# An 18-slot attention chain for the first two batches, one 512-column filler product, and weight conversions paced three then two per slot

## The chip, the cores and the metric

The kernel runs on one core of one Trainium2 chip. The metric is the device time of one execution in microseconds (us); smaller is better. The kernel before took 1901.67 us, the median of 3 runs that lie between 1897.96 and 1902.06. Engines: PE is TensorE (matmul), DVE is VectorE, ACT is ScalarE, POOL is GpSimd, SP is SyncE, which issues DMAs.

## The reference

For 8 batches of 8 heads, 576 tokens and head width 64, a Nystrom attention runs first: 32 landmarks per head are means of 18 tokens, three softmaxes (query by landmark, landmark by landmark, landmark by key), and a pseudo-inverse of the middle one by six Newton steps. Two feed-forward blocks follow on rows of 512.

```
A, Bm, C = sm(q, k_lm), sm(q_lm, k_lm), sm(q_lm, k)
for _ in range(6): Z = 2 * Z - Z @ Bm @ Z
x = (A @ Z @ C @ v)                      # heads side by side, 512 wide
u = x + (x.T @ U @ V).T ;  x = u + relu(u @ w_ch1) @ w_ch2
u = x + real(fft2(x))   ;  out = u + relu(norm(u) @ w2_ch1) @ w2_ch2
```

Each `w_ch1` is 512x2048 and each `w_ch2` is 2048x512. The weights come as 64-bit floats.

## The kernel before, in words

The two feed-forward blocks are four passes over all 8*576 columns: each pass takes half of the 2048 hidden rows. A pass goes through nine units of 512 columns. A unit has 8 "up" steps (`up`, L234) and 8 half "down" steps (L282 to L309), 16 steps in all, and every product is made of three MATMULs on a high and a low part (L241 to L243, L290 to L292). An up step ends in an ACT copy (L245) and a DVE subtraction (L246), which make the high and the low part of `g`.

The weights of the first pass are turned from 64-bit to two 32-bit parts on the chip, 16 pieces of 128x512, by `convert` (L90) under `direct` (L932). One piece has four sub-steps: (a) two DVE instructions, L96 and L97; (b) two on DVE, L100 and L103, one on ACT, L101, and one on POOL, L104; (c) one on DVE, L106, which needs L104; (d) a cast on ACT, L51, and a subtraction on POOL, L52. `direct` interleaves two pieces: a of piece n, c and d of piece n-1, b of piece n. The two small matrices U and V go through `from_f64` (L54) ahead of them, eight sub-steps.

The attention of a batch is a list of steps with slot numbers (`steps`, L664). A slot is the unit in which the kernel's code is written out: in each slot (loop at L996 before the feed-forward stream begins, loop at L1002 after it) first comes one step of the feed-forward stream or else a filler product (`filler`, L980), then the attention steps of that slot, then some conversion sub-steps. In the first loop the filler stands behind the attention steps. All engines run their instructions in the order in which they are written, so a slot is no time but a place in five queues.

Batch 0 begins at slot -21 and batch 1 at slot -10, each with 21 slots. The stream begins at slot 0. Its first unit is written in two halves and takes slots 0, 1, 2, 4, 6, 8, 9, 10; slots 3, 5 and 7 hold fillers. The second unit begins at slot 11, and from there every slot holds a stream step. Batch 2 begins at slot 4, and every later one 16 slots on.

The names that the prediction uses: `landmark` (L382, DVE L386), `kernel` and its normalisation (L410 to L428), `norms` (L434), `scores` (L458, MATMUL L468, maximum L476, exponentials L482 and L484), `query` (L527, DVE L552 and L553), `newton` (L603, L612 and L617), `rank` (L632, L641) and `mix` (L644), which gives the batch's rows, copies them (ACT L657) and splits them for the stream (ACT L51, DVE L52).

Of the kernel before, what the change touches and what calls it, by code (L numbers as in the profile page):

```python
# [20 lines left out]
B, H, S, D = 8, 8, 576, 64  # L21
DM, FF, R = 512, 2048, 32
LM, W = 32, 18
P = 128
# [15 lines left out]
def body(ctx: ExitStack, tc: tile.TileContext, qT, kT, vn, mU, mV, w11, w12, w21, w22,  # L40
         ident, bones, istack, tabs, out):
    nc = tc.nc
# [4 lines left out]
    ident_sb = const.tile([P, P], F32, name="ident_sb")  # L47
# [265 lines left out]
    STEPS = HM + 8  # L313
# [10 lines left out]
    def attention_constants(cp, t):  # L324
        nc.sync.dma_start(ident_sb, ident)
        t["U"] = cp.tile([P, 5, R], F32, name="U_sb")
        for nm in ("kb", "qb"):
            t[nm] = cp.tile([P, 4, 64], F32, name=nm)
            nc.gpsimd.memset(t[nm], 0.0)
        for nm, src, n in (("bones", bones, P), ("istack", istack, R)):  # L330
            t[nm] = cp.tile([P, n], F32, name=nm + "_sb")
            nc.sync.dma_start(t[nm], src)
        t["at"] = cp.tile([P, 4, S], F32, name="at")
        t["W"] = cp.tile([P, 4, 64], F32, name="W")
# [15 lines left out]
    def place_v(t):  # L350
        for n in range(3):
            src = t["vst"][R * n:R * n + R].unsqueeze(1).to_broadcast([R, 2, S // 3])
            for h in range(4):
                nc.sync.dma_start(t["at"][32 * h:32 * h + 32, 1 - h % 2:4:2, n * S // 3:(n + 1) * S // 3], src)

    class Batch:
# [307 lines left out]
        def steps(self, after):  # L664

            H0, H1 = slice(0, 512), slice(512, 1152)
            yield from ((2 * (nm == "q") + g, lambda nm=nm, g=g: self.landmark(nm, g)) for nm in "kq" for g in (0, 1))
            yield from ((5, self.kernel), (6, self.kernel_norm), (7, self.kernel_t), (8, self.norms), (9, self.residue))
            yield from ((10 + i, lambda i=i: self.newton(i)) for i in range(6))
            yield from ((6, self.scores), (8, lambda: self.query(0)), (9, lambda: self.query(1)),  # L670
                        (9, lambda: self.query_exp(H0)), (9, self.scores_sum), (10, lambda: self.scores_t(0)), (10, lambda: self.query(2)),
                        (11, lambda: self.scores_t(1)), (11, self.scores_tail), (11, lambda: self.query_exp(H1)),
                        (11, lambda: self.query_norm(H0)), (12, self.values), (12, lambda: self.query_norm(H1)),
                        (13, lambda: self.query_t(0)), (14, lambda: self.query_t(1)), (14, self.query_tail),
                        (15, self.mixed), (16, self.heads), (17, self.rank))
            if self.b:
                yield 13, lambda: self.mlp.get_tail(self.b)
                yield from ((15 + k // 2, lambda k=k: self.mlp.hand_tail(self.b, k)) for k in range(4))
            yield from ((19 + g, lambda g=g, n=n: self.mix(g, n)) for g in range(2) for n in range(2))
            if after:  # L680
                yield from ((r, lambda nm=nm: after.load(nm)) for r, nm in ((7, "k"), (10, "q"), (13, "v")))

        LAST = 20


    u2 = [dram.tile([DM, S], F32, name=f"u2_{b}") for b in range(B)]
# [30 lines left out]
    class Mixer:  # L717
# [170 lines left out]

        LAST = 28

    def pool(name, **k):
        return tc.tile_pool(name=name, bufs=1, reuse_waits="tile", **k)

    def chained(gens):
        for g in gens:
            yield from g

    def some(gen, n):
        for _ in range(n):
            next(gen, 0)  # L900

    class Slots:
# [5 lines left out]
        def add(self, first, steps):  # L908
            for r, step in steps:
                self.at.setdefault(first + r, []).append(step)  # L910
# [14 lines left out]
    def staging(cv, p, bufs=1):  # L925
        return chained([stage(cv, srcs[p][i], staged[p][i], bufs) for i in range(2 * HM)])

    N = NCH * STEPS
    with pool("mm") as mp, pool("pm", space=PSUM) as pm:
# [37 lines left out]
        with pool("aa") as ap_, pool("ac") as ac, pool("cv0") as cv0, pool("pt", space=PSUM) as psb:  # L967
            t = {}
            batches = [Batch(ap_, psb, t, b, mlp) for b in range(B)]
            slots = Slots()  # L970
            FIRST, GAP = -1 - Batch.LAST, 11
            half = (0, 1, 2, 4, 6, 8, 9, 10)
            for b in range(B):
                slots.add(GAP + STEPS * (b - 1) - 23 + 2 * (b == 1) if b else FIRST, batches[b].steps(batches[b + 1] if b + 1 < B else None))
            slots.add(GAP + STEPS * (B - 1) - 10, [(0, lambda: mlp.get_tail(B))])
            slots.add(GAP + STEPS * (B - 1) - 8, ((k, lambda k=k: mlp.hand_tail(B, k)) for k in range(4)))

            slots.add(FIRST, [(11, lambda: place_v(t))])

            def filler():  # L980

                ps = mlp.bank()
                for _ in range(6):
                    nc.tensor.matmul(ps[:, 0:P], ident_sb, ident_sb, start=True, stop=True)  # L984

            with tc.manual_schedule():
                for what in "kq":
                    batches[0].load(what)
                attention_constants(ac, t)
                small, large = attention_setup(t, ap_, cv0), direct()  # L990
                some(small, 1)
                some(large, 1)
                batches[0].load("v")
                some(large, 1)
                convs = chained([small, large])
                for s in range(FIRST, 0):  # L996
                    slots.run(s)
                    if s > FIRST + 5:
                        filler()
                    some(convs, 0 if s < FIRST + 4 else 1 + s % 2)  # L1000
                later, gen = staging(cv0, 1, 2), mlp.stream(0)
                for s in range(N + GAP - 8):  # L1002
                    if s >= GAP or s in half:
                        next(gen)
                    else:
                        filler()
                    slots.run(s)
                    if s < GAP + 13:
                        some(convs, 2)
                        if s == GAP + 12:  # L1010
                            some(convs, 99)
                    else:
                        some(later, 1 if s % 3 == 2 else 2)
                some(later, 999)
                some(gen, 9)
        with tc.manual_schedule(), pool("cv") as cv:
            with pool("fp") as fp, pool("fc") as fc, pool("pf", space=PSUM) as psb:
                f = {}
                slots = Slots()
# [97 lines left out]
```

## Time and profile before

| | |
|---|---|
| median of 3 runs | 1901.67 us |
| the profiled execution | 1898.48 us, of which 1896.7 us is the span from first to last instruction |
| PE busy | 1855.9 us (98%) |
| DVE, ACT, POOL busy | 914.0, 567.6, 377.4 us |
| mean granted clock of PE | 0.996 |

PE is busy nearly everywhere; its slices fall below 9 tenths at the start alone (the first slice, 47 us long, has 6). DVE is the other way round: its slices are 7, 8, 8, 6 in the first 190 us and then 6 or less. A place with a name helps to read the start: the first MATMUL of the second unit (L241, slot 11), which begins 112.73 us into the span.

### The profile page before, as it was taken

To read this page: it belongs to the slowest core of one execution; us is meant where nothing else is said; L and a number is where in the kernel's file an instruction comes from. 1 tells how busy PE (TensorE), PEld (TensorE's weight loads), DVE (VectorE), ACT (ScalarE), POOL (GpSimd) and SP (SyncE) were. 2 spreads that over 40 slices of the span, in tenths; PEclk is the share of its full clock that TensorE was granted. 3 is DMA by queue.
4 is the path that set the end of the run, shared out by engine and by line. 5 is a ranking of instruction groups with operands and counts; after the bars stand their busy time and mean duration, and the time that the engine had idled before them with its cause. 6 is when DMAs were issued, how large, how long until landed. Compare 5 with 4: busy or idle time off the path is not lost.

```text
span 1896.7 us, 30003 instructions
## 1 busy us (share of the span) xinstructions
PE 1855.9 (98%) x12184; PEld 1501.5 (79%) x12184; DVE 914.0 (48%) x1592; ACT 567.6 (30%) x1211; POOL 377.4 (20%) x354
## 2 busy tenths in 40 slices
PE   6999999999999999999999999999999999999998
PEld 5767777777788888887887888888888888888887
DVE  7886556556323434755645455464332133333333
ACT  3544443444212212323333243342322212111111
POOL 2333211221200222313222031332111000000000
PEclk9999999999999999999999999999999999999999
DMA  7454445442537343524536544252433733333332
GB/s 261 138 176 159 141 170 190 148 154 99 178 128 272 119 136 112 173 95 157 191 106 243 182 133 163 90 170 83 132 109 121 229 94 95 95 100 100 95 100 78
DMA packets 152922, 270.91 MB, mean 143 GB/s; under 512 B 23920, under 2 KB 82896, under 8 KB 152784
## 3 DMA queue, kind: packets, MB, share of 16 engines
q1 hardware_dynamic: 148176, 259.56, 40.8%
q10 hardware_dynamic: 4608, 9.44, 1.3%
q8 instruction: 95, 1.56, 0.3%
q14 instruction: 43, 0.35, 0.1%
HBM read 173.72 MB, written 94.63 MB: 141 GB/s over the span
## 4 chain that ended last, share of the span: by engine, by line
PE 88%; DVE 5%; DMA 2%; ACT 2%; issue 1%; SPq 0%; POOL 0%; ACTq 0%; DVEq 0%
PE ps L290 14%; PE ps L292 13%; PE ps L291 13%; PE ps L241 12%; PE ps L243 12%; PE ps L242 12%; PE ps_f L76 1%; DMA U<-x 1%; PE ps_f L77 1%; PE ps_f L78 1%; PE ps_c L541 1%; DVE g L246 1%; PE ps L984 1%; PE ps_l L833 1%; PE ps_n L612 1%
## 5 line engine op out<-in xcount | busy, mean ns | idle before, releaser
L241 PE MATMUL ps<-x,w 128*128 128x512 f32 x1152 | 458.3, 398 | 0.0
L290 PE MATMUL ps<-g,w 128*128 128x512 f32 x1152 | 457.5, 397 | 0.0
L292 PE MATMUL ps<-g,w 128*128 128x512 f32 x1152 | 449.6, 390 | 0.8 <-DVE g L246 0.6
L243 PE MATMUL ps<-x,w 128*128 128x512 f32 x1152 | 449.9, 391 | 0.0
L242 PE MATMUL ps<-x,w 128*128 128x512 f32 x1152 | 449.6, 390 | 0.0
L291 PE MATMUL ps<-g,w 128*128 128x512 f32 x1152 | 449.1, 390 | 0.0
L246 DVE SCALAR_TENSOR_TENSOR g<-ps,g 128x512 fp32r<-128x512 f32 x288 | 198.5, 690 | 481.2 <-ACT g L245 480.5
L245 ACT ACTIVATE g<-ps 128x512 fp32r<-128x512 f32 x288 | 171.9, 597 | 681.1 <-PE ps L243 680.5
L290 PEld LDWEIGHTS ps<-g,w 128*128 128x128 f32 x1152 | 216.2, 188 | 50.4 <-issue 5.3
L292 PEld LDWEIGHTS ps<-g,w 128*128 128x128 f32 x1152 | 216.2, 188 | 48.1 <-DVE g L246 2.0
L243 PEld LDWEIGHTS ps<-x,w 128*128 128x128 f32 x1152 | 216.6, 188 | 46.5
L241 PEld LDWEIGHTS ps<-x,w 128*128 128x128 f32 x1152 | 216.6, 188 | 45.6 <-issue 0.2
L242 PEld LDWEIGHTS ps<-x,w 128*128 128x128 f32 x1152 | 217.0, 188 | 43.1
L291 PEld LDWEIGHTS ps<-g,w 128*128 128x128 f32 x1152 | 216.5, 188 | 42.9
L52 POOL TENSOR_TENSOR x<-xf,x 128x512 fp32r<-128x512 f32 (+7 forms) x72 | 88.2, 1233 | 565.4 <-ACT x L51 536.6
L300 DVE TENSOR_TENSOR xf<-ps,xf 128x512 f32<-128x512 f32 x112 | 77.3, 690 | 239.3 <-PE ps L292 214.5
L104 POOL TENSOR_TENSOR cvp<-cvp,cva 128x512 f32<-128x512 f32 x64 | 85.6, 1338 | 425.0 <-DVE cvp L103 412.1
L52 POOL TENSOR_TENSOR stg<-cva,stg 128x512 fp32r<-128x512 f32 x48 | 68.3, 1423 | 95.4 <-ACT stg L51 95.1
L51 ACT CAST x<-xf 128x512 fp32r<-128x512 f32 (+7 forms) x144 | 76.7, 575 | 0.2
L101 ACT ACTIVATE wraw<-wraw 128x512 f32<-128x512 f32 x56 | 37.9, 677 | 123.4 <-DVE cva L97 123.4
L52 DVE TENSOR_TENSOR x<-xf,x 128x512 fp32r<-128x512 f32 (+7 forms) x72 | 51.9, 721 | 28.6 <-ACT x L51 26.1
L106 DVE SCALAR_TENSOR_TENSOR cva<-wraw,cvp 128x512 f32<-128x512 f32 x56 | 49.3, 881 | 20.7 <-POOL cvp L104 20.7
(294 smaller groups left out, 1684.0 us busy)
## 6 DMA issues: line engine op xcount, KB each, us to landing
wraw<-w SPq DMA_DIRECT2D x56, 512.0 KB
d<-stg SPq DMA_DIRECT2D x48, 512.0 KB
w<-d SPq DMA_DIRECT2D x48, 512.0 KB
y<-xf SPq DMA_DIRECT2D x76, 256.0 KB
xf<-y SPq DMA_DIRECT2D x76, 256.0 KB
u<-u1T ACTq DMA_DIRECT2D x32, 288.0 KB
U<-x SPq DMA_DIRECT2D x8, 1152.0 KB
u<-U SPq DMA_DIRECT2D x8, 1152.0 KB
```

The lines of the kernel that those rows point to most:

```text
L51: nc.scalar.copy(hi, src)
L52: (eng or nc.vector).tensor_tensor(lo, src, f32(hi), op=ALU.subtract)
L104: nc.gpsimd.tensor_tensor(pf, pf, af, op=ALU.add)
L241: nc.tensor.matmul(ps, wh, xh, start=k == 0, stop=False)
L242: nc.tensor.matmul(ps, wl, xh, start=False, stop=False)
L243: nc.tensor.matmul(ps, wh, xl, start=False, stop=k == 3)
L245: nc.scalar.activation(g[:, 0, :], ps, AF.Relu)
L246: nc.vector.scalar_tensor_tensor(out=g[:, 1, :], in0=ps, scalar=0.0, in1=f32(g[:, 0, :]), op0=ALU.max, op1=ALU.subtract)
L290: nc.tensor.matmul(ps, wh, gh, start=k == m0, stop=False)
L291: nc.tensor.matmul(ps, wl, gh, start=False, stop=False)
L292: nc.tensor.matmul(ps, wh, gl, start=False, stop=k == m1 - 1)
L300: nc.vector.tensor_tensor(res[d], ps, res[d], op=ALU.add)
```

## The change

Batches 0 and 1 take their steps from a new list, `quick`, with 18 slots instead of 21: the landmark products share a slot with nothing, but normalisation and scores share one, the third Newton step stands in the slot of the second, `mixed` comes ahead of the second half of the query transposes, and `mix` follows `rank` directly. Batch 0 now begins at slot -18 and batch 1 at slot -7; both still end at slots -1 and 10, and the stream begins at slot 0 as before. The filler becomes one MATMUL of 512 columns (the identity read four times) instead of six of 128. There are 12 of them ahead of slot 0, where there were 15. The conversions begin one place earlier in the chain and run three sub-steps a slot for five slots and then two, where they ran alternately one and two; ahead of slot 0 that makes 35 sub-steps instead of 26. From slot 0 on there are two a slot in both.

```diff
+            if self.b < 2:
+                yield from self.quick(after, H0, H1)
+                return
...
+        def quick(self, after, H0, H1):
+
+            yield from ((4, self.kernel), (5, self.kernel_norm), (5, self.scores), (6, self.kernel_t), (7, self.norms),
...
+            yield from ((16 + g, lambda g=g, n=n: self.mix(g, n)) for g in range(2) for n in range(2))
+            yield from ((r, lambda nm=nm: after.load(nm)) for r, nm in ((7, "k"), (10, "q"), (12, "v")))
+
+        QUICK, LAST = 17, 20
...
-            FIRST, GAP = -1 - Batch.LAST, 11
+            FIRST, GAP = -1 - Batch.QUICK, 11
...
-                slots.add(GAP + STEPS * (b - 1) - 23 + 2 * (b == 1) if b else FIRST, batches[b].steps(batches[b + 1] if b + 1 < B else None))
+                slots.add(FIRST + GAP * b if b < 2 else GAP + STEPS * (b - 1) - 23, batches[b].steps(batches[b + 1] if b + 1 < B else None))
...
-            slots.add(FIRST, [(11, lambda: place_v(t))])
+            slots.add(FIRST, [(10, lambda: place_v(t))])
...
-                for _ in range(6):
-                    nc.tensor.matmul(ps[:, 0:P], ident_sb, ident_sb, start=True, stop=True)
+                nc.tensor.matmul(ps, ident_sb, ident_sb.unsqueeze(1).to_broadcast([P, 4, P]), start=True, stop=True)
...
-                    some(convs, 0 if s < FIRST + 4 else 1 + s % 2)
+                    some(convs, 0 if s < FIRST + 3 else 3 if s < FIRST + 8 else 2)
```

On DVE, in the first batch's chain between the maximum of the scores (L479) and the norms (L439), the difference reads as follows. `g` is the buffer that holds a raw weight piece here, `wraw` the raw V.

```order
+L72 SCALAR_TENSOR_TENSOR u1T<-wraw,cvp 96x192
+L96 TENSOR_SCALAR cva<-g 128x512
+L97 SCALAR_TENSOR_TENSOR cva<-g,cva 128x512
 L427 STREAM_TRANSPOSE BT<-ry 128x64
 L428 TENSOR_REDUCE st<-BT 128x2
 L430 TENSOR_TENSOR dg<-istack_sb,st 128x128
-L65 TENSOR_SCALAR cvp<-cva 96x192
-L68 SCALAR_TENSOR_TENSOR cvp<-wraw,cvp 96x192
+L100 TENSOR_SCALAR cvp<-cva 128x512
+L103 SCALAR_TENSOR_TENSOR cvp<-g,cvp 128x512
+L96 TENSOR_SCALAR cva<-g 128x512
+L97 SCALAR_TENSOR_TENSOR cva<-g,cva 128x512
```

The first weight pieces stand here now, where V stood, and sub-step a of a piece (L96, L97) follows directly on b of the piece before it (L100, L103).

On DVE in the first unit, between two Newton steps of batch 1 (L617), `wraw` is now a raw weight piece:

```order
 L100 TENSOR_SCALAR cvp<-cva 128x512
 L103 SCALAR_TENSOR_TENSOR cvp<-g,cvp 128x512
+L96 TENSOR_SCALAR cva<-wraw 128x512
+L97 SCALAR_TENSOR_TENSOR cva<-wraw,cva 128x512
 L246 SCALAR_TENSOR_TENSOR g<-ps,g 128x512
 L617 TENSOR_TENSOR ry<-ry,ps_n 128x2x32
 L552 TENSOR_REDUCE sm<-ps_b 128x4
 L553 TENSOR_TENSOR A<-ps_b,sm 128x128
-L96 TENSOR_SCALAR cva<-g 128x512
-L97 SCALAR_TENSOR_TENSOR cva<-g,cva 128x512
 L106 SCALAR_TENSOR_TENSOR cva<-g,cvp 128x512
```

Before, b and a stood in different slots with attention between them; with the change a pair b, a stands together in every second slot.

On ACT, at batch 0's `mix` (L657 copies its rows, L51 with `x` splits them), the exponentials of batch 1's scores (L482, L484) move behind the first pair of splits:

```order
 L661 DMA u_0_62<-u1T 128x576
 L51 CAST x<-u1T 128x512
+L482 ACTIVATE E,st<-ps_c,st 128x512
+L484 ACTIVATE E,st<-ps_b,st 128x64
+L482 ACTIVATE E,st<-ps_c,st 128x512
+L484 ACTIVATE E,st<-ps_b,st 128x64
+L51 CAST w_240<-cva 128x512
 L657 COPY u1T<-ps_n 128x288 x2
 L657 COPY u1T<-ps 128x288 x2
```

Four exponentials and a weight cast now stand between the two halves of `mix`; before, they stood ahead of both.

## Rows read from the trace of the kernel before

**Rows 1.** Windows by stage: length, each engine's busy us (xinstructions), PE clock, DMA share, GB/s

```profile
0.00:12.43 12.43, 1.05 (x24) 0.72 (x32) 6.51 (x8) 1.63 (x2) 3.78 (x15) 1.00 0.75 245
12.43:66.79 54.36, 48.01 (x903) 39.12 (x901) 42.15 (x102) 26.00 (x71) 14.97 (x18) 0.94 0.61 216
66.79:112.73 45.94, 41.03 (x524) 29.82 (x522) 40.41 (x80) 22.83 (x58) 20.75 (x22) 0.96 0.48 162
112.73:179.90 67.17, 65.86 (x744) 48.77 (x741) 50.33 (x102) 29.68 (x74) 23.56 (x25) 0.97 0.46 155
```

**Rows 2.** Timeline of PE: start us, us, engine, line, operation [idle before, releaser]

```profile
109.98 2.23 PE L468 MATMUL ps_c<-k__897,qb 64*32 64x512 f32 x16 [2.87 <-ACT u1T L657]
112.73 0.80 PE L241 MATMUL ps<-x,w 128*128 128x512 f32 x1
113.32 0.63 PE L242 MATMUL ps<-x,w 128*128 128x512 f32 x1
116.51 0.39 PE L241 MATMUL ps<-x,w 128*128 128x512 f32 x1
176.73 1.09 PE L468 MATMUL ps_c<-k__1701,qb 64*32 64x512 f32 x16
238.87 1.09 PE L468 MATMUL ps_c<-k__2502,qb 64*32 64x512 f32 x16
```

**Rows 3.** Timeline of DVE, waits of the first stretch

```profile
25.86 0.69 DVE L552 TENSOR_REDUCE sm<-ps_c 128x16 f32<-128x512 f32 x1 [3.44 <-PE ps_c L541]
61.57 1.29 DVE L52 TENSOR_TENSOR x<-u1T,x 128x512 fp32r<-128x512 f32 x2 [2.34 <-ACT x L51]
65.50 1.29 DVE L52 TENSOR_TENSOR x<-u1T,x 128x512 fp32r<-128x512 f32 x2
```

**Rows 4.** Timeline of DVE, the conversion of a weight piece

```profile
28.10 0.69 DVE L97 SCALAR_TENSOR_TENSOR cva<-g,cva 128x512 uint32<-128x512 uint32 x1
29.37 0.42 DVE L100 TENSOR_SCALAR cvp<-cva 128x512 uint32<-128x512 uint32 x1
29.82 0.69 DVE L103 SCALAR_TENSOR_TENSOR cvp<-g,cvp 128x512 f32<-128x512 uint32 x1
30.43 0.42 DVE L96 TENSOR_SCALAR cva<-g 128x512 uint32<-128x512 uint32 x1
30.89 1.64 DVE L97 SCALAR_TENSOR_TENSOR cva<-g,cva 128x512 uint32<-128x512 uint32 x1
35.66 0.68 DVE L106 SCALAR_TENSOR_TENSOR cva<-g,cvp 128x512 f32<-128x512 f32 x1
```

**Rows 5.** Windows, batch 1's kernel_t, and its norms with query(0)

```profile
56.29:57.03 0.74, 0.74 (x11) 0.62 (x13) 0.67 (x5) 0.56 (x1) 0.00 (x0) 1.00 1.00 399
62.78:64.90 2.12, 1.78 (x84) 1.65 (x85) 1.98 (x8) 1.98 (x5) 0.00 (x0) 1.00 0.43 154
```

**Rows 6.** Timeline of POOL

```profile
30.66 1.32 POOL L104 TENSOR_TENSOR cvp<-cvp,cva 128x512 f32<-128x512 f32 x1 [11.93 <-DVE cvp L103]
59.09 1.29 POOL L52 TENSOR_TENSOR w<-cva,w 128x512 fp32r<-128x512 f32 x1 [7.75 <-ACT w L51]
```

**Rows 7.** Windows of line L97 alone: DVE busy us (xinstructions), PE clock, DMA share, GB/s

```profile
12.43:66.79 54.36, 5.36 (x5) 0.94 0.61 216
66.79:112.73 45.94, 4.44 (x5) 0.96 0.48 162
```

**Rows 8.** Timeline of DVE, one L100 in the first unit

```profile
76.26 1.51 DVE L100 TENSOR_SCALAR cvp<-cva 128x512 uint32<-128x512 uint32 x1
```

**Rows 9.** Windows, from batch 1's first exponential to batch 0's second split

```profile
56.47:62.06 5.59, 5.12 (x107) 3.83 (x109) 3.12 (x8) 5.47 (x16) 2.52 (x2) 1.00 0.54 215
```

**Rows 10.** SP's issue of the first four weight pieces, and a window behind it

```profile
10.42 1.85 SPq L88 DMA_DIRECT2D g<-w  x4
...
14.00:16.00 2.00, 2.00 (x30) 1.65 (x22) 1.74 (x7) 0.00 (x0) 0.00 (x0) 1.00 1.03 393
```

**Rows 11.** Timeline of PE, one filler

```profile
20.07 1.60 PE L984 MATMUL ps<-ident_sb 128*128 128x128 f32 x12
```

More of the change, by code (lines that the diff above doesn't have):

```diff
@@ L681, in steps @@
                 yield from ((r, lambda nm=nm: after.load(nm)) for r, nm in ((7, "k"), (10, "q"), (13, "v")))
-        LAST = 20
+        def quick(self, after, H0, H1):
+            yield from ((4, self.kernel), (5, self.kernel_norm), (5, self.scores), (6, self.kernel_t), (7, self.norms),
+                        (8, self.residue), (9, lambda: self.newton(0)), (10, lambda: self.newton(1)),
+                        (11, lambda: self.newton(3)), (12, lambda: self.newton(4)), (13, lambda: self.newton(5)))
+            yield from ((7, lambda: self.query(0)), (8, lambda: self.query(1)), (8, lambda: self.query_exp(H0)),
+                        (8, self.scores_sum), (9, lambda: self.scores_t(0)), (9, lambda: self.query(2)),
+                        (10, lambda: self.scores_t(1)), (10, self.scores_tail), (10, lambda: self.query_exp(H1)),
+                        (10, lambda: self.query_norm(H0)), (10, lambda: self.newton(2)), (11, self.values),
+                        (11, lambda: self.query_norm(H1)), (12, lambda: self.query_t(0)), (12, self.mixed),
+                        (13, lambda: self.query_t(1)), (13, self.query_tail), (14, self.heads), (15, self.rank))
+            if self.b:
+                yield 11, lambda: self.mlp.get_tail(self.b)
+                yield from ((14 + k // 2, lambda k=k: self.mlp.hand_tail(self.b, k)) for k in range(4))
+            yield from ((16 + g, lambda g=g, n=n: self.mix(g, n)) for g in range(2) for n in range(2))
+            yield from ((r, lambda nm=nm: after.load(nm)) for r, nm in ((7, "k"), (10, "q"), (12, "v")))
+        QUICK, LAST = 17, 20
     u2 = [dram.tile([DM, S], F32, name=f"u2_{b}") for b in range(B)]
```

## The prediction

> **What bounds the kernel now.** I read the page first: PE is busy 98% of the span, so the change can only win or lose where PE is not full, and the slices put that at the start. Then windows by stage [rows 1], cut at three instructions that both kernels have: DVE's maximum of the first kernel scores at 12.43, the end of DVE's last split of batch 0 at 66.79 (the stream's first unit can be finished only after it), and the first MATMUL of the second unit at 112.73. The reader is to see that behind 112.73 PE is idle for 1.3 of 67.2 us, so whatever moves that MATMUL moves the end. Ahead of it DVE is the fullest engine beside PE: 42.15 of 54.36 us in the second window and 40.41 of 45.94 in the third. PE looks full there too, but it holds fillers, and the timelines show it waiting for DVE and ACT. Last I read the timeline of DVE for what its idle time consists of [rows 3] and for the price of a conversion [rows 4]; the order of the changed kernel gives the counts.
>
> I call the windows A (to 12.43), B (to 66.79), C (to 112.73) and D (the second unit). A has the same work in both kernels.
>
> **B, up to the last split of batch 0.** DVE works 42.15 us and is idle 12.2 us in it. By the order, the change puts 7 sub-steps a, 6 b and 6 c ahead of the last split; before there were 5, 4 and 4. One piece costs DVE 0.42+0.69+0.42+0.69+0.68 = 2.90 us [rows 4], so two pieces more are 5.8 us. Batch 1 is three slots less far: its kernel_t, norms and first query product leave the window, 0.67+1.98 = 2.65 us of DVE [rows 5].
>
> The third item is a collision. L97 takes 0.69 us [rows 4], but the one at 30.89, right behind b of the piece before, took 1.64: POOL's L104 had begun at 30.66 and ran until 31.98 [rows 6], and L97 ended half a microsecond later. That is 0.95 us lost. In B before, the five L97 took 5.36 us together [rows 7], so two of them were hit (5 x 0.69 + 2 x 0.95). The change puts a directly behind b for six of its seven. From none to all six may be hit: a pair escapes when POOL is held up, as in front of 59.09, where its L52 had waited for ACT [rows 6] and L104 stood behind it. I take five, since in the new order L52 stands half a chain ahead of the next L104: 5 x 0.95 - 1.9 = 2.85 us more (bounds -1.9 and +3.8). DVE's work in B becomes 42.15 + 5.8 - 2.65 + 2.85 = 48.15 us.
>
> Of the idle 12.2 us, the wait of 3.44 at 25.86 [rows 3] goes, because conversions now fill the place where PE was late; so do most of the small ones. One comes: at the end of B the exponentials of batch 1 stand on ACT between the two halves of `mix`. From the first exponential to the end of the second split ACT was busy 5.47 of 5.59 us [rows 9]. In the new order this chain starts when DVE has its maximum, and DVE has only one L106 (0.68) to do beside it, then waits for the split; one conversion pass in that row is no longer in the chain, so I put this wait at 4.2 us (it was 2.34 at 61.57 [rows 3]). With 2.8 us for waits that stay (the start of `scores`, `rank`, the first split), idle is 7 us, with bounds of 4 and 11. B is then 55.15 us, 0.8 longer (bounds -7.0 and +5.7).
>
> The first weight piece is read earlier than before, at about 17 us by the DVE work that stands ahead of it. The four first pieces are issued from 10.42 on, and 2.1 MB at 393 GB/s [rows 10] are some 5.3 us, so the first is there and the fourth is just in time. A wait of up to 2 us here is inside the bound on idle. On SP the ninth piece's load moves ahead of batch 2's k, and the copies of V into `at` and batch 1's v move by one slot; their readers stand a third of a chain further on, so I cost them at nothing, and up to 1 us if one of them lands late, again inside that bound. Fillers: one took 1.60 us [rows 11]; the new one lies between 0.39 (a 512-column MATMUL of the stream [rows 2]) and 1.60. In B they lie beside DVE's work, so that gain is nothing.
>
> **C, the first unit with the chain of batch 1.** DVE worked 40.41 us and was idle 5.5. To it come batch 1's 2.65 us and one sub-step a (0.42 + 0.69 = 1.1); b and c are 6 and 5 in both. All six L97 now follow a b directly. Before, the five took 4.44 us [rows 7], one of them hit; also an L100 took 1.51 instead of 0.42 beside a POOL subtraction [rows 8], which the new pairing (c with d, b with a) avoids. Five hits of six: 4.75 - 0.98 - 1.09 = 2.7 us more (bounds -2.1 and +4.7). DVE's work: 40.41 + 2.65 + 1.1 + 2.7 = 46.9 us, more than the whole window had. PE was busy 41.03 of 45.94; it gets the products of those steps of batch 1 (at most the 2.5 us it was busy in rows 5) and loses up to 3 x 1.2 us of filler, so it does not become the longer one. Idle of DVE shrinks but does not vanish, as it still waits for ACT between `mix` and the second unit: 3.5 us (bounds 2 and 5.5). C is 50.4 us, 4.4 longer (bounds -1.8 and +8.4).
>
> **D, the second unit.** From L468 to L468 it takes 66.75 us and the next unit 62.14 [rows 2]. Of these 4.6 us, 1.14 are L468 itself (2.23 against 1.09), which lies ahead of 112.73. The rest, 3.4 us, is what fewer conversions in D could give back at most. Part of it is the clock: the window 12.43 to 66.79 shows 0.94 and D shows 0.97 [rows 1], and behind the idle 2.87 us ahead of 109.98 the MATMULs take 0.63 instead of 0.39 us [rows 2], the lower of the two levels. That wait for ACT is in the changed kernel too. I take 1.0 us (bounds 0 and 3.4).
>
> **Sum.** 0.8 + 4.4 - 1.0 = 4.2 us. On the profiled execution, 1898.48, that makes 1902.7; that execution lies 3.2 us under the median of the runs, 1901.67, so the forecast is 1905.9 us. The three slots that are gone cost DVE nothing before, and what stood in them does not go away.
>
> **Rivals.**
>
> *The idle time is won back.* Idle in B shrinks to its bound of 4 us and pairs are hit only once there (port term -0.95): 42.15 + 5.8 - 2.65 - 0.95 + 4 = 48.35, 6.0 shorter. In C no pair is hit: 40.41 + 2.65 + 1.1 - 2.1 + 3.5 = 45.6, 0.3 shorter. With 1.0 from D the sum is -7.3, 1894.4 us. For it: 12.2 us idle in B is large, and 3.44 of it was a wait for PE alone. Against it: an L97 behind a b was hit whenever POOL was free, and ACT's chain at `mix` grows. It decides if POOL's L104 begins after L97 in most pairs.
>
> *The terms cancel.* Half of the pairs are hit (B 0.6 shorter, C 2.5 longer), and D gives 2: 1901.7 us. For it: the two windows are full by different engines, so a shift of work from one to the other is paid once. Against it: the sum of DVE's work ahead of 112.73 grows by 6.9 us before any collision.
>
> *Every pair is hit, and idle stays.* Six hits in each window (0.95 more in B and in C), idle 9 in B and 5 in C: B 58.1 (+3.7), C 52.8 (+6.9), D nothing: +10.6, 1912.3 us. For it: PE would then wait more often between products, and each step of 12 MATMULs at the lower clock level costs up to 12 x 0.24 = 2.9 us. Against it: two of the twelve pairs stand where ACT holds POOL up. The Trainium skill (SBUF — State Buffer, Who interferes with whom) states this as a rule: DVE and GpSimd share one port pair under an exclusive lock, and a DVE instruction with two SBUF inputs waits out a GpSimd instruction that reads SBUF. The trace agrees at 30.89 (1.64 us), and by that rule all twelve pairs would pay.
>
> **How the numbers follow.** Forecast 0.42, idle won back 0.20, cancelled 0.20, every pair 0.18. The likeliest case alone runs from 1901 to 1910. From 1895 to 1913 us about half of the first and half of the last rival stay outside, 2 in 10. A difference under 0.2%, 3.8 us, cannot be told from no change by a measurement of this kernel. Faster by more than that: the first rival and a little of the second, 0.22. Within it: most of the second and two fifths of the forecast, 0.35. Slower: the rest, 0.43.
>
> **What would show it.** In the changed profile the last of the four first-batch splits (L52 with `u1T`) should end near 67.6, after a DVE wait of some 4 us for ACT L51 behind the exponentials. L97 should take about 1.6 us for ten of the first thirteen. The second unit's first L241 should come near 118, and the unit should last about 65.5 us from L468 to L468. The prediction is wrong if the last split ends ahead of 62, if most L97 behind a b take 0.69, or if the second unit begins ahead of 112.7.

## The result, and the profile after

The changed kernel takes 1914.65 us (median of 4 runs, 1913.29 to 1915.31) against 1900.32 us of the kernel before beside it (4 runs): ratio 1.0075, 95% interval 1.0058 to 1.0093. It is slower. The forecast was 1905.9 us with a range up to 1913; the sign was right and the size too small. The profiled execution took 1915.11 us with a span of 1913.3, 16.6 us more than before, and these 16.6 us are explained here (the medians differ by 14.3; the profiled execution of the kernel before was one of its faster ones).

The windows of the changed kernel, cut at the same instructions as [rows 1] (the last one here ends at the next unit's L468):

```profile
0.00:12.12 12.12, 1.04 (x24) 0.72 (x32) 6.55 (x9) 1.63 (x2) 3.82 (x15) 1.00 0.77 250
12.12:72.02 59.90, 44.55 (x606) 21.45 (x604) 47.98 (x103) 27.97 (x74) 22.24 (x22) 0.86 0.61 213
72.02:124.63 52.61, 46.47 (x634) 31.61 (x632) 45.01 (x86) 23.45 (x58) 19.94 (x21) 0.87 0.42 131
124.63:193.35 68.72, 63.98 (x707) 47.84 (x701) 41.82 (x87) 26.65 (x69) 17.69 (x21) 0.95 0.42 139
```

The third number group is DVE. In B it worked 47.98 us, where 48.15 were forecast, and was idle 11.9, where 7 were forecast. PE's timeline answers to [rows 2]:

```profile
122.97 1.36 PE L468 MATMUL ps_c<-k__992,qb 64*32 64x512 f32 x16 [0.78 <-ACT u1T L657]
...
124.63 0.50 PE L241 MATMUL ps<-x,w 128*128 128x512 f32 x1
...
132.46 0.46 PE L437 MATMUL ps_b<-dg,bones_sb 128*128 128x128 f32 x2 [2.10 <-DVE dg L430]
...
193.35 1.09 PE L468 MATMUL ps_c<-k__1633,qb 64*32 64x512 f32 x16
```

The last split of batch 0 ends 5.2 us later than before (72.02 against 66.79), the second unit's first L241 comes 11.9 later (124.63 against 112.73), and the next unit's L468 16.6 later (193.35 against 176.73). So by these three places B lost 5.2, C 6.7 and D 4.7 us (B's own length grew by 5.5, as A is 0.3 shorter); the next L468 comes 62.1 us later in both, so nothing is lost or won after that. DVE's waits in B, answering to [rows 3]:

```profile
31.07 0.22 DVE L617 TENSOR_TENSOR ry<-ry,ps_n 128x64 f32<-128x64 f32 x1 [0.80 <-ACT ry L616]
39.09 0.22 DVE L617 TENSOR_TENSOR ry<-ry,ps_n 128x64 f32<-128x64 f32 x1 [1.11 <-ACT ry L616]
41.55 0.29 DVE L524 TENSOR_TENSOR Y<-ps_b,st 128x128 f32<-128x128 f32 x1 [1.55 <-PE ps_b L519]
57.11 0.60 DVE L641 COPY W<-ps_n 32x128 f32<-32x128 f32 x2 [1.23 <-ACT W L641]
62.64 1.29 DVE L52 TENSOR_TENSOR x<-u1T,x 128x512 fp32r<-128x512 f32 x2 [1.60 <-ACT x L51]
70.73 1.29 DVE L52 TENSOR_TENSOR x<-u1T,x 128x512 fp32r<-128x512 f32 x2 [3.99 <-ACT x L51]
```

The wait of 3.44 us for PE is gone and the wait at `mix` is 3.99 (forecast 4.2). But three waits for ACT copies (L617 twice, L641) take 3.14 us together, where the kernel before had one of 0.38. What ACT did there, and at a place in C and three in D, is seen in its own timeline:

```profile
30.31 0.62 ACT L51 CAST w<-cva 128x512 fp32r<-128x512 f32 x1 [5.16 <-DVE cva L106]
30.83 0.21 ACT L616 COPY ry<-ps_n 128x64 f32<-128x64 f32 x1
...
38.84 0.21 ACT L616 COPY ry<-ps_n 128x64 f32<-128x64 f32 x1 [0.21 <-PE ps_n L612]
...
55.91 0.62 ACT L51 CAST w<-cva 128x512 fp32r<-128x512 f32 x1 [1.62 <-DVE cva L106]
56.55 0.52 ACT L641 COPY W<-ps_n 32x128 f32<-32x128 f32 x2
...
79.19 0.62 ACT L51 CAST w<-cva 128x512 fp32r<-128x512 f32 x1 [5.90 <-DVE cva L106]
79.71 0.59 ACT L245 ACTIVATE g<-ps 128x512 fp32r<-128x512 f32 x1
...
138.85 0.62 ACT L51 CAST w<-cva 128x512 fp32r<-128x512 f32 x1 [6.95 <-DVE cva L106]
147.78 0.62 ACT L51 CAST w<-cva 128x512 fp32r<-128x512 f32 x1 [3.45 <-DVE cva L106]
158.60 0.62 ACT L51 CAST w<-cva 128x512 fp32r<-128x512 f32 x1 [6.94 <-DVE cva L106]
```

and in DVE's timeline of the place in C:

```profile
78.47 0.68 DVE L106 SCALAR_TENSOR_TENSOR cva<-g,cvp 128x512 f32<-128x512 f32 x1
80.34 0.69 DVE L246 SCALAR_TENSOR_TENSOR g<-ps,g 128x512 fp32r<-128x512 f32 x1 [1.18 <-ACT g L245]
```

In these rows ACT keeps the order of its queue. The cast of sub-step d waited for sub-step c (L106), which DVE does last in the same slot; L616, L641 or L245, for which the rows show no wait of their own, stood behind it; and then DVE waited for them. Of the three waits in B two are of this kind (0.80 and 1.23 us); the third, 1.11 at 39.09, ended with PE's L612, a little later than the cast. In D the pattern comes three times, each wait of DVE 1.18 us. The length of such a wait is no sign by itself: in D of a run without the pattern (e8, below) DVE waits 1.14 us for L245 too, but there L245 had waited 2.74 us for PE.

### The profile page after: what moved, and what is told of

Its sections match the earlier page's. It is cut to its first block, busy times and chain, and to the rows that moved or that the text cites. A ratio compares the mean times of both kernels' runs of the same rounds, so it can differ in the third digit from the quotient of the medians.

```text
span 1913.3 us, 29635 instructions
## 1 busy us (share of the span) xinstructions
PE 1859.0 (97%) x11998; PEld 1486.7 (78%) x11998; DVE 919.0 (48%) x1592; ACT 567.4 (30%) x1211; POOL 378.7 (20%) x354
## 4 chain that ended last, share of the span: by engine, by line
PE 84%; DVE 9%; DMA 3%; ACT 2%; issue 1%; SPq 0%; POOL 0%; ACTq 0%; DVEq 0%; POOLq 0%
PE ps L290 13%; PE ps L292 13%; PE ps L291 13%; PE ps L241 12%; PE ps L243 12%; PE ps L242 12%; PE ps_f L76 1%; DMA U<-x 1%; PE ps_f L77 1%; PE ps_f L78 1%; DVE g L246 1%; DVE cva L97 1%; DVE cva L106 1%; PE ps_l L853 1%; PE ps_b L519 1%
## 5 line engine op out<-in xcount | busy, mean ns | idle before, releaser
L241 PE MATMUL ps<-x,w 128*128 128x512 f32 x1152 | 459.3, 399 | 2.8 <-ACT x L51 2.7
L245 ACT ACTIVATE g<-ps 128x512 fp32r<-128x512 f32 x288 | 171.9, 597 | 667.5 <-PE ps L243 667.0
L241 PEld LDWEIGHTS ps<-x,w 128*128 128x128 f32 x1152 | 217.0, 188 | 50.0 <-ACT x L51 3.1
L52 POOL TENSOR_TENSOR x<-xf,x 128x512 fp32r<-128x512 f32 (+7 forms) x72 | 88.2, 1233 | 562.4 <-ACT x L51 534.2
L104 POOL TENSOR_TENSOR cvp<-cvp,cva 128x512 f32<-128x512 f32 x64 | 87.3, 1364 | 433.7 <-DVE cvp L103 433.4
L52 POOL TENSOR_TENSOR stg<-cva,stg 128x512 fp32r<-128x512 f32 x48 | 68.3, 1423 | 95.9 <-ACT stg L51 95.6
L51 ACT CAST x<-xf 128x512 fp32r<-128x512 f32 (+7 forms) x144 | 76.7, 576 | 0.2
L52 DVE TENSOR_TENSOR x<-xf,x 128x512 fp32r<-128x512 f32 (+7 forms) x72 | 52.7, 733 | 29.1 <-ACT x L51 27.4
L106 DVE SCALAR_TENSOR_TENSOR cva<-wraw,cvp 128x512 f32<-128x512 f32 x56 | 49.3, 880 | 21.3 <-POOL cvp L104 21.3
```

The lines of the kernel that those rows point to most:

```text
L51: nc.scalar.copy(hi, src)
L52: (eng or nc.vector).tensor_tensor(lo, src, f32(hi), op=ALU.subtract)
L104: nc.gpsimd.tensor_tensor(pf, pf, af, op=ALU.add)
L241: nc.tensor.matmul(ps, wh, xh, start=k == 0, stop=False)
L245: nc.scalar.activation(g[:, 0, :], ps, AF.Relu)
```

## The new theory, and its rivals

The kernel before has 26 conversion sub-steps ahead of slot 0, the changed one 35. The sub-steps come as a, c, d, b, two to a slot (three in the first five slots of the new pace). An even count pairs them (a, c), (d, b); an odd one (c, d), (b, a), and from slot 0 on nothing corrects it. **Theory 1** is that the odd pairs are the cause: (b, a) makes L97 collide with POOL's L104, (c, d) blocks ACT's queue. **Theory 2**: more conversion work ahead and batch 1 three slots less far. **Theory 3**: the short fillers let TensorE's clock fall (B shows 0.86 instead of 0.94). Below, C and D are cut at L468 of the second unit and of the next, B begins behind the maximum at 12.43 (0.23 us long) instead of with it, and the table, worked out from the windows of each profile, gives DVE's busy time in B too.

```
kernel              ratio to before  [interval]        B us (DVE)     C us    D us
before              1                                  54.13 (41.92)  43.19   66.72
changed             1.0075 [1.0058, 1.0093]            59.67 (47.76)  50.95   70.33
e1_even             1.0009 [1.0000, 1.0018]            56.02 (46.45)  44.06   64.50
e8_even_late        1.0019 [1.0010, 1.0028]            58.27 (47.73)  44.36   64.48
e2_before_odd       1.0051 [1.0037, 1.0065]            55.67 (42.08)  48.20   70.28
e3_swap             1.0064 [1.0051, 1.0077]            57.52 (44.97)  49.78   68.83
e9_d_late           1.0035 [1.0022, 1.0048]            58.59 (48.14)  48.89   64.77
e11_both            1.0058 [1.0046, 1.0071]            58.54 (45.92)  48.54   68.97
e16_raw3            1.0063 [1.0050, 1.0076]            59.83 (47.74)  49.34   68.71
e15_both_raw3       1.0026 [1.0016, 1.0037]            57.54 (46.00)  44.64   66.17
e4_old_filler       1.0076 [1.0064, 1.0089]            59.63 (47.80)  50.44   68.63
e13_before_two      1.0030 [1.0019, 1.0042]            59.74 (50.61)  43.08   66.77
e5_chain_alone      1.0156 [1.0143, 1.0170]            53.33 (35.79)  54.55   87.09
e10_late_scores     0.9997 [0.9988, 1.0006]            52.16 (44.76)  47.51   64.51
e14_two_late        0.9990 [0.9981, 0.9999]            48.86 (41.59)  48.92   64.47
e17_two_28          1.0002 [0.9993, 1.0010]            52.29 (44.04)  47.81   66.25
```

## Experiments: the pairs

**e1_even**, 34 sub-steps in the changed kernel:

```diff
-some(convs, 0 if s < FIRST + 3 else 3 if s < FIRST + 8 else 2)
+some(convs, 0 if s < FIRST + 3 else 3 if s < FIRST + 7 else 2)
```

> Edit: the changed kernel, with one conversion sub-step fewer in the eighth slot (three per slot for four slots, then two), so 34 sub-steps instead of 35 stand ahead of slot 0, and from there on each slot holds the pairs (a, c) and (d, b), as before the change, instead of (c, d) and (b, a). Theory 1, the pairs: with (b, a) L97 runs into POOL's L104 (1.65 instead of 0.69 us), and with (c, d) ACT's cast of d stands ahead of L245 and waits for DVE's L106; the odd count made both. Then nearly all of what the second and third window and the second unit lost against my forecast comes back: about 10 us under the changed kernel (1904.5, from 1901 to 1908), L97 is hit in at most 3 of the first 13, and the waits of DVE for ACT L245 of 1.18 us vanish. Theory 2, the amount: more conversions ahead and the second batch three slots less far; one sub-step fewer gives its own 0.7 to 1.1 us and no more (1913 to 1914). Theory 3, TensorE's clock and the fillers: no change (1914.7).

Measured: 1899.82 us beside a before of 1898.46. One sub-step fewer gives 12.5 us or so (0.66%), as theory 1 said and theory 2 could not; three of the first thirteen L97 (at 20.08, 43.95 and 50.64) are hit. The median lies under theory 1's range of 1901 to 1908; by its ratio on the 1900.32 of the result it is 1902.0, inside it. B, C and D all gain. In B the same 102 DVE instructions stand as in the changed kernel, and B is 3.65 us shorter, 1.3 of it DVE's work and 2.3 its idle time.

**e8_even_late**, the pairs turned only from slot 0 on:

```diff
-... else 3 if s < FIRST + 8 else 2)
+... else 3 if s < FIRST + 8 else 2 - (s == -1))
```

> Edit: the changed kernel, with one sub-step instead of two in the last slot ahead of slot 0 only (34 in all). The pairs of the second window stay (c, d) and (b, a), those from slot 0 on become (a, c) and (d, b). Theory 1: the last split of batch 0 ends near 72 us as in the changed kernel, and the third window and the second unit win 7 us together (4 hits of L97 at 0.95 and some 3 us of waits for L245 and L616 behind the cast in the one, the waits of 1.18 us in the other): 1907.5, from 1904 to 1910. Theory 2: 1913 to 1914. Theory 3: 1914.7.

Measured: 1902.41 us beside 1898.46. Its windows B, C and D:

```profile
12.29:70.56 58.27, 44.15 (x606) 21.05 (x591) 47.73 (x103) 28.09 (x74) 22.03 (x22) 0.79 0.61 218
70.56:114.92 44.36, 40.87 (x602) 28.24 (x600) 41.23 (x83) 22.24 (x56) 18.27 (x21) 0.96 0.46 151
114.92:179.40 64.48, 63.76 (x732) 46.57 (x732) 42.91 (x89) 28.43 (x72) 18.56 (x22) 0.97 0.46 152
```

C wins 6.6 us and D 5.9, more than the 7 expected together, and the median lies under theory 1's range too. And here ACT does L245 ahead of its cast, which finds its input done:

```profile
77.00 0.60 ACT L245 ACTIVATE g<-ps 128x512 fp32r<-128x512 f32 x1 [4.71 <-PE ps L243]
77.49 0.62 ACT L557 ACTIVATE A<-A 128x512 f32<-128x512 f32 x1
78.01 0.61 ACT L51 CAST w<-cva 128x512 fp32r<-128x512 f32 x1
```

**e2_before_odd**, the kernel before with one sub-step more:

```diff
-some(convs, 0 if s < FIRST + 4 else 1 + s % 2)
+some(convs, 0 if s < FIRST + 4 else 1 + s % 2 + (s == -1))
```

> Edit: the kernel before the change, with one conversion sub-step more in the last slot ahead of slot 0 (27 instead of 26), so that from slot 0 on the pairs are (c, d) and (b, a); the chain, the fillers and the pace before that are the old ones. Theory 1: the last split of batch 0 stays near 66.8 us, and the third window and the second unit lose what they lost in the changed kernel by the pairs: 6 to 9 us, 1908 (from 1905 to 1910), with L97 at 1.65 us in most of the pairs and waits of DVE for L245 near 1.2 us. Theory 2: one sub-step more ahead, 0.3 to 1.1 us (1901). Theory 3: no change (1900.3).

Measured: 1908.59 us beside 1898.46, ratio 1.0051. The last split ends at 67.72, 0.9 later than before; C and D lose 5.0 and 3.6 us:

```profile
67.72:115.92 48.20, 39.76 (x491) 30.16 (x489) 39.31 (x74) 21.45 (x56) 21.38 (x22) 0.96 0.41 137
115.92:186.20 70.28, 65.95 (x736) 48.51 (x737) 50.07 (x99) 30.41 (x76) 24.35 (x26) 0.95 0.45 156
```

DVE's work in C grew by 0.6 us only (38.68 to 39.31); its idle time grew from 4.5 to 8.9. The time lies in theory 1's range. So the odd pairs, without any other part of the change, cost two thirds of what the change costs. What follows from the three runs: theory 1 stands for C and D.

## Experiments: what in the odd pairs costs the time

**e3_swap**, a ahead of b; only the collision goes:

```diff
-for g in (new, old, old, new):
+for g in (new, old, old, old):
```

> Edit: the changed kernel, with a of the next piece issued ahead of b within their slot instead of behind it; the pairs (c, d) and (a, b) and their slots stay, and with them ACT's cast behind L106. Only the collision goes. Theory 1 has two parts, and this tells them apart. If the collision is the larger: the eight hits of the first thirteen L97 and the three of the second unit go, at 0.95 us each some 6 us in the second and third window, less what stays hidden: 1908 to 1910. If the cast behind L106 is the larger, DVE only waits longer for L245 and L616: 1912.5 to 1914.5. Theory 2 and 3: 1914.7, no change.

Measured: 1910.76 us beside 1898.46 (ratio 1.0064: some 2 us of the change's 14 come back by the ratios, 3.9 by the medians; the intervals of the two ratios overlap). The median lies between the ranges of the two readings. All L97 take 0.69, and C and D win 1.2 and 1.5 us only: with the collision alone taken away, a fifth of what e8 wins there. A part of the gain is spent in the same windows: DVE now waits 3.99 us, in five waits of L96, for the load of a raw piece (`wraw`), where the changed kernel had one of 0.38 us.

**e9_d_late**, the cast's input a pair earlier, the collision kept (an empty step stands in place of the first d, so that the pairs stay odd):

```diff
-for g in (new, old, old, new):
+for g in (new, older, old, new):
...
-old = new
+older, old = old, new
```

> Edit: the changed kernel, with sub-step d of a piece moved back by one pair, so that c of a piece now shares its slot with d of the piece before (d first); 34 real sub-steps stand ahead of slot 0, and b is still directly followed by a. The collision of L97 with POOL stays, and ACT's cast finds its L106 done. The run with a ahead of b took the collision away alone and won 3.9 us (2.3 in the second window, 1.2 in the third, 1.6 in the second unit, with 0.7 lost or not resolved), the run with the old pairs from slot 0 on won 6.6 in the third window and 5.9 in the second unit. Theory 1a, the cast behind L106 holds ACT's queue and is the larger part: the third window and the second unit win some 9 to 10 us here though L97 is hit in most pairs, and the waits of DVE for ACT L245 are gone: 1903.5, from 1901 to 1906. Theory 1b, the collision is the larger part and the waits for L245 only follow from it: at most 3 us, 1910 to 1913.

Measured: 1906.87 us beside 1899.73 (ratio 1.0035), 0.9 us over the range of theory 1a and well under that of 1b. D is at 64.77, all of its loss gone, though three L97 in it take 1.66 us. So in D it is the cast. C wins 2.1 us only, where more was expected, with DVE waiting for a load:

```profile
100.03 1.08 DVE L96 TENSOR_SCALAR cva<-wraw 128x512 uint32<-128x512 uint32 x1 [0.95 <-DMA wraw<-w]
108.70 1.11 DVE L96 TENSOR_SCALAR cva<-wraw 128x512 uint32<-128x512 uint32 x1 [1.21 <-DMA wraw<-w]
```

**e11_both**, both edits (the line shown against e9):

```diff
-for g in (new, older, old, new):
+for g in (new, old, older, old):
```

> Edit: both edits together, a ahead of b and d one pair later; the count of sub-steps ahead of slot 0 and the slots in which a, b and c stand stay as in the changed kernel. Alone they won 2.3 and 1.3 us in the second window, 1.2 and 2.1 in the third (to L468), 1.6 and 5.6 in the second unit. Theory 1, in which collision and cast explain the odd pairs: the last split ends near 69 us, the second unit keeps 64.8 us, and the sum, 11 to 13 us, is reached: 1901 to 1903. Rival: the odd pairs hold a third cost. In the run with d late, two L96 waited 0.95 and 1.21 us for the load of wraw, which can start only when c of the piece before last has read its buffer; this is not touched here, so the third window wins no more than 3.5 of the 6.6 us that the old pairs won there: 1903 to 1906.

Measured: 1911.42 us beside 1900.13 (ratio 1.0058): a miss for both readings, worse than e9. Without the first two delays DVE reaches L96 earlier than its data. The waits for `wraw` are now 10.0 us in six; DVE's timeline shows the step:

```profile
96.38 0.69 DVE L106 SCALAR_TENSOR_TENSOR cva<-wraw,cvp 128x512 f32<-128x512 f32 x1
...
100.93 0.43 DVE L96 TENSOR_SCALAR cva<-wraw 128x512 uint32<-128x512 uint32 x1 [2.33 <-DMA wraw<-w]
```

and SP issues the load as soon as L106 has read its buffer, at 97.07:

```profile
97.13 0.33 SPq L88 DMA_DIRECT2D wraw<-w  x1
```

There are two `wraw` buffers, so the load of piece n+1 waits for c of piece n-1, and in the odd pairs a of piece n+1 stands in the next slot. In e8 the same load had 4.4 us (issued at 96.05, read at 100.48) and nothing waited.

**e16_raw3** and **e15_both_raw3**, a third raw buffer, borrowed from `stg`, in the changed kernel and in e11:

```diff
-raw = cv0.tile([P, 1024], U32, name="wraw", bufs=2)
+raw = cv0.tile([P, 1024], U32, name="wraw", bufs=2) if i % 3 != 2 else f32(cv0.tile(
+    [P, 2, 512], F32R, name="stg", bufs=1)).rearrange("p a n -> p (a n)").bitcast(U32)
```

> Edit: the changed kernel with the third raw buffer alone. Its only wait of L96 for wraw was 0.38 us, at 104.27. If the load stands hidden behind the other two parts, the time stays at 1912.5 to 1914.7. If it holds up more than the waits of DVE show, 2 us or more come back: 1909 to 1912.

> Edit: the run with both edits (a ahead of b, d one pair later), and every third of the later pieces loaded into the buffer that the staging uses later, so that three raw buffers take turns and a load need not wait for c of the piece before last. If the load of wraw is the third part of what odd pairs cost, the six waits of L96 (10.0 us) go, the third window comes to 44 to 45.5 us and the second unit to 64.8: 1900 to 1903. Rival: something else in the odd order is late behind it, and DVE waits elsewhere: 1906 to 1911.

Measured: e16 1911.97 us (ratio 1.0063), 2.3 us by the ratios, whose intervals overlap, so whether the load holds up anything by itself is not shown; e15 1904.06 (1.0026), between the ranges of its two readings, both beside 1899.29. On top of the other two edits the third buffer wins 6 us (e11 1.0058, e15 1.0026), clear of the noise. With all three parts gone C and D are

```profile
70.09:114.73 44.64, 39.84 (x602) 27.14 (x600) 41.15 (x84) 22.34 (x56) 18.71 (x20) 1.00 0.47 150
114.73:180.90 66.17, 63.90 (x732) 47.22 (x732) 43.04 (x88) 28.75 (x73) 19.79 (x23) 0.97 0.45 148
```

against 44.36 and 64.48 with the even pairs. So for C the three parts are the whole loss (6.3 of 6.6 us), for D 4.2 of 5.9. Alone they win 1.2, 2.1 and 1.6 in C: 4.9 of 6.3 us, each near what two equal windows differ by (1.4 us, see the end). Taking away two uncovers the third: the load is worth more behind the other two edits than alone. What is left in D (1.7 us against e8, and against e9, which has less taken away) was not followed further.

## Experiments: the rest of the change

**e4_old_filler**:

```diff
-nc.tensor.matmul(ps, ident_sb, ident_sb.unsqueeze(1).to_broadcast([P, 4, P]), start=True, stop=True)
+for _ in range(6):
+    nc.tensor.matmul(ps[:, 0:P], ident_sb, ident_sb, start=True, stop=True)
```

> Edit: the changed kernel with the old filler, 6 MATMULs of 128 columns instead of one of 512; nothing else. Theory 3 (the shorter filler lets TensorE's granted clock fall, and the products behind it are slow): the granted clock of the second window rises from 0.86 to 0.94 and 3 us or more come back (1909 to 1911). Theory 1: the fillers stand beside DVE's work, and the time stays within 1 us (1912 to 1914 beside a kernel before of 1898.5, which is where the changed kernel stands by its ratio).

Measured: 1914.00 us beside 1899.73 (ratio 1.0076). B's granted clock rises to 0.91, its length stays at 59.63. Theory 3 falls: the fillers cost and win nothing.

**e13_before_two**, the kernel before with 34 sub-steps ahead:

```diff
-some(convs, 0 if s < FIRST + 4 else 1 + s % 2)
+some(convs, 0 if s < FIRST + 4 else 2)
```

> Edit: the kernel before the change with 34 sub-steps ahead of slot 0 (two in each of the 17 slots instead of one and two by turns), so the pairs are (a, c) and (d, b) throughout; its chain and fillers are the old ones. It asks what more conversions ahead cost or win by themselves. If each piece ahead of the last split costs its DVE time, two pieces more are 5.8 us in the second window, of which the third window gives back what its own pieces took: 1900 to 1904. If DVE's idle 12 us of that window take them in, the window stays at 54 to 55 us and the third wins: 1894 to 1898.

Measured: 1905.84 us beside 1900.13 (ratio 1.0030), above the range of either reading. B is as long as in the changed kernel:

```profile
12.11:71.85 59.74, 50.33 (x903) 41.27 (x888) 50.61 (x111) 27.87 (x75) 20.42 (x22) 0.89 0.56 196
```

DVE works 8.7 us more (two pieces are 5.8; among the rest, L103's mean rose from 0.69 to 0.86) and the window is 5.6 longer, so idle takes in a third of it; C and D stay as they were (43.08 and 66.77). Two pieces more in B buy nothing later; in D, too, DVE works 6.2 us less (43.02 against 49.27) and the window is no shorter. Theory 2 has its share here: B's 5 us.

**e5_chain_alone**, the changed chain with the old pace and the old filler, 22 sub-steps ahead:

```diff
-some(convs, 0 if s < FIRST + 3 else 3 if s < FIRST + 8 else 2)
+some(convs, 0 if s < FIRST + 4 else 1 + s % 2 + (s == -1))
```

> Edit: the 18-slot chain alone, with the old pace of the conversions (22 sub-steps ahead of slot 0, an even count as before the change) and the old filler. It puts 12 to 13 sub-steps fewer ahead of slot 0 than the changed kernel, so these come later, in the third window and the second unit. Theory 1: the old pairs are there from slot 0 on, so no waits for L245 of 1.2 us; the second window loses three pieces of 2.9 us of DVE's work against the run with 34 sub-steps, and the third window and the second unit have to take them as far as they have room: 1898, from 1894 to 1902. Theory 2 (the chain of the second batch, three slots less far, costs the time): about 1908 to 1912, as in the changed kernel.

Measured: 1929.56 us beside 1899.73 (ratio 1.0156), a miss for both. B is 6.3 us shorter than in the changed kernel, but D takes 87.09 us. PE's longest waits between 65 and 207 us (total, times, longest) say why:

```profile
PE ps L291 <- POOL w L52: 11.1, 5, 3.5
PE ps L290 <- ACT w L51: 7.7, 3, 3.8
PE ps L241 <- ACT w L51: 3.1, 1, 3.1
```

TensorE waits for converted weights. With three slots gone, the shorter chain needs a faster pace; between 22 and 28 sub-steps ahead (e17, below, which has the new filler and later scores as well) lies a cliff.

**e10_late_scores**, e1 with batch 1's scores a slot later (part of the line, shown against e1):

```diff
-(5, self.kernel_norm), (5, self.scores),
+(5, self.kernel_norm), (5 + (self.b == 1), self.scores),
```

> Edit: the run with 34 sub-steps, with the second batch's scores one slot later, so that its four exponentials stand on ACT behind the second half of mix instead of between the halves, where DVE waited 2.4 us for ACT L51 (4.0 us in the changed kernel). If the exponentials set that wait, the last split ends 2 to 3 us earlier (65 to 66 instead of 68.1), and if the second window then still decides the end, the time is 2 us less than 1899.8: 1897.5. If the third window takes it back, because the later scores stand ahead of its chain, the time stays at 1899 to 1900.5.

Measured: 1898.99 us beside 1899.73 (ratio 0.9997). B is 3.9 us shorter than in e1, since no exponentials stand between the halves of `mix` and the second split waits for nothing; C is 3.5 longer, as the scores stand there now. By the ratios some 2 us remain, with intervals that overlap.

**e14_two_late** and **e17_two_28**, e10 with two sub-steps in each slot, from the fourth slot on (e14, shown against e10) or from the fifth (e17, with `FIRST + 4`):

```diff
-some(convs, 0 if s < FIRST + 3 else 3 if s < FIRST + 7 else 2)
+some(convs, 0 if s < FIRST + 3 else 2)
```

> Edit: the run with 34 sub-steps and the late scores, with two sub-steps per slot from the fourth slot on and none of the triples (30 ahead of slot 0, an even count). One piece less ahead of the last split takes 2.9 us of DVE's work out of the second window: the last split ends at 62 us or earlier. If the weights are still there in time, the time is 1896 to 1898; if TensorE has to wait for converted weights in the third window and the second unit, as in the chain alone with 22 (waits for w of ACT L51 and POOL L52, together 22 us), a part of that comes, one piece being a quarter to a third of it: 1902 to 1907.

> Edit: the run with two sub-steps per slot and late scores, starting one slot later: 28 sub-steps ahead of slot 0 instead of 30 (an even count). Half a piece less ahead of the last split: the second window is 1.5 us shorter (59.5 instead of 61.0). If the weights are still in time, 1896 to 1897; if TensorE begins to wait for converted weights in the second unit, the time rises to 1899 to 1905.

Measured: e14 1897.75 us beside 1900.13, ratio 0.9990 with an interval of 0.9981 to 0.9999, the fastest of all; the interval ends just under 1, so a gain over the kernel before is barely told from none. Its B, C and D:

```profile
12.15:61.01 48.86, 37.36 (x605) 18.46 (x590) 41.59 (x93) 23.34 (x62) 17.46 (x19) 0.93 0.62 216
61.01:109.93 48.92, 42.52 (x603) 29.56 (x602) 42.91 (x86) 25.25 (x66) 19.50 (x22) 0.93 0.49 168
109.93:174.40 64.47, 62.40 (x733) 46.08 (x733) 46.42 (x94) 29.51 (x74) 21.50 (x24) 1.00 0.48 160
```

e17 takes 1899.88 beside 1899.29 (1.0002). Its B was expected at 1.5 us shorter and is 3.4 longer, and TensorE doesn't wait for weights in it; that miss has no explanation from these runs. One thing its profile shows is that four DVE instructions of the set-up (L61, L62, L65 and L68, 1.1 us) moved from A into B.

## Why the prediction was wrong, point by point

The sums of DVE's work came out within 2 us. What failed is DVE's idle time: forecast at 7 us in B and 3.5 in C, measured at 11.9 and 7.6. In C and D the wait that was left out is ACT's cast of sub-step d, which in the pairs (c, d) holds up what stands behind it.

- **B, DVE's work: right.** 48.15 us forecast, 47.98 measured. The collision's size was right too; L97 alone, answering to [rows 7]:

```profile
12.12:72.02 59.90, 8.63 (x7) 0.86 0.61 213
72.02:124.63 52.61, 7.96 (x6) 0.87 0.42 131
```

  That is four hits of seven and four of six (7 x 0.69 + 4 x 0.95 = 8.63), where five and five were taken. That B's sum fits so closely is luck in part: the hit that is missing, 0.95 us, is made up by two L100 of 0.83 and 1.04 us (usually 0.42), each begun while a POOL L52 ran.
- **B, the wait at `mix`: right** (4.2 forecast, 3.99 measured).
- **B, "2.8 us for waits that stay": wrong, and the first step that failed.** The listed waits other than `mix` are 6.3 us, of which 2.03 are L617 and L641 behind the blocked cast. The prediction treated DVE's idle time as room that conversions fill. In e13 added work of 8.7 us took in 3.1 us of idle, in the changed kernel 5.8 us took in 0.3. B grew by 5.5 instead of 0.8 us.
- **C, idle of "3.5 us (bounds 2 and 5.5)": wrong, the second.** Work was 45.01 (46.9 forecast), idle 7.6. The prediction saw that c now stands with d and b with a, and priced only b with a. The pairing (c, d) was counted as a gain of 1.09 us (the slow L100 it "avoids"). No L100 is slow in C any more, but the L96 at 104.27 is, by 1.06; and e8 and e9 show that the pairing blocks ACT's queue. C lost 6.7 instead of 4.4 us.
- **D, "I take 1.0 us (bounds 0 and 3.4)", a gain: wrong in sign, the third.** It lost 4.7 us from L241 on (3.6 from L468 to L468, where 65.5 were forecast and 70.4 measured). No loss was allowed for, though the pairs go on through D: e2 loses 3.6 us there by one sub-step, e9 wins them back. That fewer conversions in D give time back isn't shown either: D is 2.2 us shorter than before in e1 and e8, but not in e13, which has as little conversion work there.
- **The rival "every pair is hit, and idle stays"** has the nearest number, 1912.3 us. Its idle half (9 and 5 us) was nearer than the forecast, its collision half was not the cause: 8 of the 12 pairs were hit, and with no hit at all (e3) the kernel still takes 1910.76. The rule of the Trainium skill (SBUF — State Buffer, Who interferes with whom), where the order of issue decides who blocks, agrees with the trace: L97 was held where POOL had begun first and took 0.69 us in the three pairs where it began first itself. So by that rule not all twelve pairs pay; the prediction left the order out when it said that they would. Taken away alone, the collisions are worth 2 to 4 us of the 14 here.
- **The rival "the terms cancel"** has a slip: with half of B's six pairs hit, B would be 1.1 us shorter, not 0.6; nothing hangs on it.
- **The fillers at nothing: right** (e4). **"The three slots that are gone cost DVE nothing before": right for the pace chosen**, but e5 shows what they had bought: time for weights.

So of the 16.6 us C and D have 11.4, from an odd count of sub-steps (e8 wins it back), and B has 5.2, whose cause is shown in part only. In the old chain the pieces put ahead cost as much by themselves (e13); in the new one an earlier even count wins 3.65 us of B back with the same instructions (e1), more than the 1.4 us by which two equal windows differ. How B's loss is shared among pieces, pairs and chain was not taken apart.

## What to carry to other kernels

When work is dealt out in small steps, some per slot, write down which steps share a slot before and after; a count that changes from even to odd re-pairs everything behind it. For each pair ask on every in-order queue what stands behind an instruction whose input is made last in the same slot, and what waits for that. And when one delay is taken out of such a ring, look for the next one (here the load of the raw buffer) before calling the first one cheap.

## What the runs showed of the hardware

The slow one of two colliding instructions is the one that begins second. At 46.69 the changed kernel's L97 began ahead of POOL's L104; L97 took 0.69 and L104 1.69 us, where 1.26 to 1.43 is usual. Of the twelve pairs in B and C eight have POOL first (L97 takes 1.63 to 1.65 us) and three DVE first (L97 0.69, L104 1.69 or 1.70); in the twelfth L96 was held. DVE's and then POOL's timeline:

```profile
46.69 0.69 DVE L97 SCALAR_TENSOR_TENSOR cva<-g,cva 128x512 uint32<-128x512 uint32 x1
...
104.27 1.48 DVE L96 TENSOR_SCALAR cva<-wraw 128x512 uint32<-128x512 uint32 x1 [0.38 <-DMA wraw<-w]
```

```profile
46.83 1.69 POOL L104 TENSOR_TENSOR cvp<-cvp,cva 128x512 f32<-128x512 f32 x1
...
104.21 1.26 POOL L104 TENSOR_TENSOR cvp<-cvp,cva 128x512 f32<-128x512 f32 x1
```

The second row of each shows that a DVE instruction with one tensor input is held too: L96 took 1.48 instead of 0.42 us beside L104. Unexpected was also that a stretch with the same instructions differs: B up to its last split is the same in the changed kernel and in e8, and took 59.67 and 58.27 us, so a single window is good to some 1.5 us at best. What one edit alone won in C (1.2 to 2.1 us) is near that; what the pairs together cost, and the cast in D, is far above it.
